# Linear attention and two feed-forward layers on one core: fixed instruction order from block 1 on, and work in smaller pieces

## The chip, the core and the metric

The kernel runs on one core of one Trainium2 chip. The metric is the device time of one execution in microseconds (us). A core has five engines that run side by side, each with an instruction stream of its own: TensorE (PE in the profile; its weight loads are PEld), VectorE (DVE), ScalarE (ACT), GpSimd (POOL) and SyncE (SP), which here issues transfers only. Engines wait for each other by semaphores.

## What is computed

```python
def _attn_ref(q, k, v):                      # 8 batches, 8 heads, 576 positions, 64 wide
    q_s = np.exp(q - np.max(q, axis=-1, keepdims=True))
    q_s = q_s / (np.sum(q_s, axis=-1, keepdims=True) + 1e-09)
    k_s = np.exp(k - np.max(k, axis=2, keepdims=True))
    k_s = k_s / (np.sum(k_s, axis=2, keepdims=True) + 1e-09)
    kv = np.einsum('bhsd,bhse->bhde', k_s, v)
    return np.einsum('bhsd,bhde->bhse', q_s, kv)
...
x = attention, transposed to (4608 tokens, 512)
x = maximum(x @ w_in1, 0) ** 2 @ w_out1      # w_in 512 x 2048, w_out 2048 x 512
h = x @ w_in2
x = (h / (1 + exp(-h))) @ w_out2
```

All of it is float32.

## The kernel before

**Numbers in two halves.** TensorE multiplies a rounded float32 type. To keep float32's precision every operand is split into a high part (ScalarE casts it to the rounded type) and a low part (VectorE subtracts the high part from the value), and each product is three matmuls: high x high, high x low, low x high. Splitting is the main work of ScalarE and VectorE. Weights are rounded beforehand (L170 on ScalarE; L171, L174 and L177 on VectorE, for each of two halves of a weight row block).

**Blocks.** Tokens go in nine blocks of 512 (4608 / 512). Block i runs the first matrix product, `layer_in`, in 16 slots (`for n in range(NF)`): a slot makes 128 of the 2048 hidden values with 12 matmuls into one of four PSUM banks named h. `hidden` then does relu (L580, tile g) and square (L581, tile st) on ScalarE, every fourth slot four sums of 512 columns (L567 to L570; on VectorE, in blocks 7 and 8 on GpSimd with 256 columns), and stores to DRAM (g1d). During block i the attention of block i + 1 is made, for four pairs of heads: loads, maximum over k (`kv_max`, with a reduction over partitions on GpSimd), exp of q and k, k times v on TensorE (`kv_mm`), its normalisation (`kv_norm`), q's normalisation (`q_norm`), a transposition of q through DRAM (`q_tr`: VectorE, one store to qd, four loads to qw), q's split into qh (L505, ScalarE) and ql (L506, VectorE), the product `x_mm` (tile xps, L529 to L531) and its split into xh and xl (`x_keep`). A table of slots, `side`, says in which slot each step is written.

**Phases 1 to 3.** The other three products (w_out1, w_in2, w_out2) use a scheme with seven products of half-size blocks in place of eight (PRODUCTS, with weights B11, T3, T2, T1, B21, N4, B22). A weight set (`seven`) is made for each of 8 row blocks: loads, four subtractions (L240 to L243) and seven splits (L249 on ScalarE, L250 on VectorE). Phase 1's sets are made during the blocks, those of phases 2 and 3 during the last unit of the phase ahead; phases 2 and 3 read weights that `round_to_dram` has rounded and stored meanwhile. A phase has five units, four of two blocks (512 columns) and one of one block (256), in the order 0, 1, 2, 4, 3 in phases 1 and 2. A unit is 56 steps (7 products x 8 row blocks) of six matmuls (`step`, `mm3`). Inputs are loaded 14 steps ahead and split six steps ahead (`stream`: `a_load`, `a_split`, tiles al and ah). In phase 2 each group of seven steps ends in PSUM banks a, b, c and d, read out by `after`: L748 (u + b) and L749 (c + u) after the third product, L752 after the fourth, and so on, then silu, sums and stores. The matmul of product N4, the sixth, adds to bank c again and so has to wait for L749.

**What sets the order.** The kernel is written as a Python program whose statements give the source order. A scheduler then places each engine's instructions; it starts from the source order and lets an instruction pass another where it expects the other to wait. SBUF is handed out as 89 rooms of 128 x 512 (`room`, `back`), and a room that is given back goes to the end of a queue.

## Time and profile before

| | |
|---|---|
| median of 3 runs | 1740.39 us (1737.68 to 1742.43) |
| the profiled execution | 1736.66 us |
| its span, first to last instruction | 1734.9 us |
| TensorE / VectorE / ScalarE / GpSimd busy | 91% / 71% / 50% / 21% of the span |
| mean granted TensorE clock | 0.960 of full speed |

The profile is one execution. Its clock column tells what share of full speed TensorE was granted; the records show two levels, 1.00 (2.4 GHz) and 0.5 (1.2 GHz). Block 0 ends 105 us after the start, block 8 at 584, phase 1 at 965, phase 2 at 1382, phase 3 at 1728.

### The profile page before, as it was taken

What the parts mean: (1) busy time and instruction counts of PE and PEld (TensorE: products, weight loads), DVE (VectorE), ACT (ScalarE), POOL (GpSimd) and SP (SyncE); (2) the same over time, 40 slices, a digit from 0 to 9 for tenths busy, and PEclk for the clock granted to TensorE, in tenths of its full rate; (3) what the DMA queues carried; (4) which work ended last, traced back from release to release, by engine and by line L of the source; (5) the groups of instructions that cost most, each with busy time, mean ns of one, the idle gap of its engine ahead of it and who ended that gap; (6) DMA issues with size and microseconds to landing.
All of it is one profiled execution on the core that took longest, in us unless ns stands there. A gap on an engine that the chain in (4) does not pass through costs nothing. (4 is left out here: it accounts for less than half of the span.)

```text
span 1734.9 us, 25646 instructions
## 1 busy us (share of the span) xinstructions
PE 1587.0 (91%) x7624; PEld 1286.3 (74%) x7624; DVE 1227.1 (71%) x2490; ACT 876.0 (50%) x1981; POOL 369.9 (21%) x628
## 2 busy tenths in 40 slices
PE   6899988989989999999989698989999899999998
PEld 3678766767767788878867477767887688888888
DVE  8876765766677766567677778787778875656565
ACT  7866555555456644444455435343344554444433
POOL 2000000000047600000031343444566600000000
PEclk9999988989989999999899899999999999999999
DMA  8757666666577778796887468677676977776846
GB/s 232 232 191 236 204 193 212 190 217 216 173 255 243 254 255 305 239 322 199 285 271 252 160 236 289 231 272 260 227 241 221 304 233 195 241 239 196 245 130 168
DMA packets 291915, 401.77 MB, mean 232 GB/s; under 512 B 67072, under 2 KB 215296, under 8 KB 290752
## 3 DMA queue, kind: packets, MB, share of 16 engines
q1 hardware_dynamic: 264592, 293.95, 54.8%
q0 software_dynamic: 25824, 105.66, 16.2%
q8 instruction: 61, 1.00, 0.2%
q10 hardware_dynamic: 1360, 0.52, 0.1%
q14 instruction: 78, 0.64, 0.1%
HBM read 226.23 MB, written 173.80 MB: 231 GB/s over the span
## 5 line engine op out<-in xcount | busy, mean ns | idle before, releaser
L671 DVE TENSOR_TENSOR al<-al,ah 128x512 fp32r<-128x512 f32 (+1 forms) x630 | 385.0, 646 | 215.8 <-ACT ah L670 201.8
L670 ACT CAST ah<-al 128x512 fp32r<-128x512 f32 (+1 forms) x630 | 338.6, 576 | 214.5 <-DVE al L671 74.6
L681 PE MATMUL a<-ah,wB 128*128 128x512 f32 (+1 forms) x960 | 288.2, 370 | 7.8 <-ACT u L746 4.1
L555 PE MATMUL h<-xh,wih 128*128 128x512 f32 x576 | 235.7, 415 | 20.2 <-ACT wih L201 8.5
L557 PE MATMUL h<-xh,wil 128*128 128x512 f32 x576 | 234.6, 409 | 1.2 <-DVE wil L202 1.1
L556 PE MATMUL h<-xl,wih 128*128 128x512 f32 x576 | 234.0, 407 | 0.7 <-DVE xl L546 0.7
L681 PEld LDWEIGHTS a<-ah,wB 128*128 128x128 f32 x960 | 176.3, 190 | 39.7 <-ACT u L746 5.2
L681 PE MATMUL c<-ah,wN 128*128 128x512 f32 (+1 forms) x480 | 152.0, 386 | 46.6 <-DVE st L749 46.4
L681 PE MATMUL a<-al,wB 128*128 128x512 f32 (+1 forms) x480 | 178.1, 371 | 0.7 <-DVE al L671 0.6
L681 PE MATMUL d<-ah,wT 128*128 128x512 f32 (+1 forms) x480 | 149.0, 378 | 3.6 <-ACT ah L670 3.5
L555 PEld LDWEIGHTS h<-xh,wih 128*128 128x128 f32 x576 | 113.1, 198 | 51.2 <-ACT xh L545 13.6
L681 PE MATMUL b<-ah,wT 128*128 128x512 f32 (+1 forms) x480 | 146.1, 373 | 3.6 <-ACT ah L670 3.6
L681 PE MATMUL d<-ah,wB 128*128 128x512 f32 (+1 forms) x480 | 147.6, 377 | 0.0
L681 PE MATMUL c<-ah,wT 128*128 128x512 f32 (+1 forms) x480 | 144.7, 369 | 1.5 <-ACT ah L670 1.4
L681 PEld LDWEIGHTS c<-ah,wN 128*128 128x128 f32 x480 | 89.9, 193 | 74.1 <-DVE st L749 56.5
L170 ACT ACTIVATE wraw<-wraw 128x256 int32<-128x256 uint32 x128 | 53.8, 433 | 165.6 <-DMA wraw<-in_moe_w_in_dram 96.2
L580 ACT ACTIVATE g<-h 128x512 f32<-128x512 f32 x144 | 84.6, 594 | 99.1 <-PE h L557 89.8
L557 PEld LDWEIGHTS h<-xh,wil 128*128 128x128 f32 x576 | 113.1, 196 | 27.0 <-DVE wil L202 2.8
L556 PEld LDWEIGHTS h<-xl,wih 128*128 128x128 f32 x576 | 113.6, 197 | 24.8 <-DVE xl L546 1.0
L681 PEld LDWEIGHTS d<-ah,wT 128*128 128x128 f32 x480 | 91.2, 196 | 20.0 <-ACT ah L670 4.9
L739 ACT ACTIVATE st<-st 128x512 f32<-128x512 f32 (+1 forms) x120 | 70.4, 586 | 70.3 <-DVE st L752 28.6
L681 PEld LDWEIGHTS a<-al,wB 128*128 128x128 f32 x480 | 91.0, 190 | 18.0 <-DVE al L671 3.0
(143 smaller groups left out, 2856.3 us busy)
## 6 DMA issues: line engine op xcount, KB each, us to landing
al<-g1d SPq DMA_DIRECT2D x224, 256.0 KB, 5.2
al<-g2d SPq DMA_DIRECT2D x224, 256.0 KB, 3.4
g1d<-st SPq DMA_DIRECT2D x56, 896.0 KB, 4.3
g2d<-st POOLq DMA_DIRECT2D x64, 512.0 KB, 3.4
g2d<-st POOLq DMA_DIRECT2D x112, 256.0 KB, 3.7
wraw<-in_moe_w_in_dram SPq DMA_DIRECT2D x64, 256.0 KB, 4.8
wraw<-in_moe_w_out_dram SPq DMA_DIRECT2D x64, 256.0 KB, 4.3
g1d<-st POOLq DMA_DIRECT2D x16, 896.0 KB, 5.0
```

The costliest lines, as they stand in the source:

```text
L170: nc.scalar.activation(lw, lw.bitcast(U32), AF.Copy, scale=2.0 ** -29)
L555: nc.tensor.matmul(h, wih[f][:, o], xh[i, c], start=(c == 0), stop=False)
L556: nc.tensor.matmul(h, wih[f][:, o], xl[i, c], start=False, stop=False)
L557: nc.tensor.matmul(h, wil[f][:, o], xh[i, c], start=False, stop=(c == KC - 1))
L580: nc.scalar.activation(g, h, AF.Relu)
L670: nc.scalar.copy(hi[:, o], f32(lo)[:, o])
L671: nc.vector.tensor_tensor(lo[:, o], f32(lo)[:, o], f32(hi)[:, o], op=ALU.subtract)
L681: nc.tensor.matmul(p, a, b, start=first and m == 0, stop=last and m == 2, skip_group_check=cont)
L739: nc.scalar.activation(at_(s), at_(s), AF.Silu)
```

## The change

Three things are changed. A wrapper around each engine marks every instruction that is written from block 1 on so that it keeps the source's order on its engine (block 0 and what is ahead of it are left to the scheduler). Attention's steps are cut at the change of engine (`kv_sub` from `kv_exp`, `kv_low` from `kv_norm`, `q_max` from `q_exp`, `q_back` from `q_tr`, `q_low` from `q_split`, `x_low` from `x_keep`) and a table gives each piece its slot; side steps are written ahead of `hidden` of their slot. Weight sets and the roundings to DRAM are generators that give up control after every half rounded, every two subtractions and every split, so that their pieces come one to a slot or step; when they begin is set anew (`WHEN`, and limits on free rooms less those owed). Each engine has the same number of instructions of each kind as before.

```diff
+    class InOrder:
...
+            def call(*a, **kw):
+                got = fn(*a, **kw)
+                if pinned[0] and got is not None:
+                    tc.keep_in_program_order(got)
+                return got
...
-    def rounded(ph, raw, add=None):
+    def rounding(ph, raw, to):
         u = room(F32, "wu")
         for h, t in enumerate(raw):
...
-        back(*raw)
+            back(t)
+            yield
...
-    def round_to_dram(ph, f, raw):
-        u = rounded(ph, raw)
-        nc.gpsimd.dma_start(out=wd[ph, f], in_=u)
-        back(u)
+    def round_to_dram(ph, f):
+        raw = raw_load(ph, f)
+        owed[0] += 1
+        for _ in range(8 if ph == 2 else 4):
+            yield
+        to = []
+        owed[0] -= 1
+        yield from rounding(ph, raw, to)
+        yield
+        gp.dma_start(out=wd[ph, f], in_=to[0])
+        back(to[0])
...
     def seven(ph, x, engine):
...
         engine.tensor_tensor(t1, b12, b11, op=ALU.subtract)
         engine.tensor_tensor(t3, b22, b12, op=ALU.subtract)
+        yield
         engine.tensor_tensor(t2, b22, t1, op=ALU.subtract)
         engine.tensor_tensor(n4, b21, t2, op=ALU.subtract)
-        yield
+        for _ in range(1 if ph == 1 else 4):
+            yield
...
             W[ph, x, n] = w[name]
-            if n == 3:
-                yield
+            yield
...
+    ORDER = (
...
+        (q_tr, 4, 3), (q_back, 4, 4), (kv_norm, 4, 5), (kv_low, 4, 6), (q_split, 5, 7),
+        (q_low, 5, 8), (x_mm, 6, 9), (x_keep, 6, 10), (x_low, 6, 11),
+    )
...
-        for pr, s in enumerate((0, 3, 6, 9) if i == 0 else (-6, -2, 2, 6)):
+        for pr, s in enumerate((0, 3, 6, 9) if i == 0 else (-8, -4, 0, 4)):
...
-    WHEN = [(2, 4), (4, 4), (6, 4), (7, 4), (7, 10), (8, 0), (8, 5), (8, 10)]
+    WHEN = [(1, 8), (3, 8), (5, 8), (7, 0), (7, 0), (7, 8), (8, 0), (8, 4)]
...
+            pinned[0] = i > 0
             h = layer_in(i, fs[n])
...
+            if i > 0:
+                for fn, a in side.get((i, n), ()):
+                    fn(*a)
             hidden(i, n, h)
...
-            if making is not None and (i >= B - 1 or n % 2 == 0):
-                making = None if next(making, 0) == 0 else making
+            if late or n % 2 == 0:
+                making[:] = [x for x in making if next(x, 0) != 0]
...
-    while n1 < NG or making is not None:
-        if making is None:
-            making = seven(1, n1, nc.gpsimd)
+    while n1 < NG or making:
+        if n1 < NG and len(making) < 2 and len(rooms) >= 13 + 11 * len(making):
+            making.append(seven(1, n1, gp))
             n1 += 1
-        making = None if next(making, 0) == 0 else making
+        making[:] = [x for x in making if next(x, 0) != 0]
...
-            a, b = ((n % 14 == 3, n % 14 == 10) if ph == 1 else (
-                (j < NG - 2 and x == 2), (0 < j < NG - 1 and x == 1)
-            ))
...
+        if ph < 3 and not done and nw[ph + 1] < NF and len(rooms) - owed[0] >= 3 and (
+            n % 13 == 3 if ph == 1 else ((u != LAST_LONG[0] or j > 2) and j < NG - 2 and x == 0)
+        ):
+            doing.append(round_to_dram(ph + 1, nw[ph + 1]))
```

What it does to the order is shown at three places. In these rows the changed kernel's line is always L73, the wrapper's; the instruction is known by its tiles. wraw, wu and wt are tiles of the weight rounding and of a set's subtractions; wB, wT and wN are parts of a weight set.

The first is ScalarE in the blocks. Before, in the stretch that ran from 337.67 us, around the end of block 4:

```order
L170 ACTIVATE wraw<-wraw 128x256 x3
L249 CAST wB_3829<-wu 128x256
L170 ACTIVATE wraw<-wraw 128x256
L580 ACTIVATE g<-h 128x512
L581 ACTIVATE st<-g 128x512
L249 CAST wB_3950<-wu 128x256
L249 CAST wB_3944<-wu 128x256
L249 CAST wT_3838<-wt 128x256
L249 CAST wT_3832<-wt 128x256
L249 CAST wT_3835<-wt 128x256
L372 ACTIVATE kvs<-kvps,rc 64x64
L505 CAST qh<-qw 128x512
```

The changed kernel at the end of block 4, where the same weight set gets its first split:

```order
L73 CAST qh<-qw 128x512
L73 ACTIVATE g<-h 128x512
L73 ACTIVATE st<-g 128x512
L73 ACTIVATE g<-h 128x512
L73 ACTIVATE st<-g 128x512
L73 CAST wB_3961<-wu 128x256
L73 ACTIVATE kvs<-kvps,rc 64x64 x2
L73 ACTIVATE q<-q 128x512
L73 ACTIVATE g<-h 128x512
L73 ACTIVATE st<-g 128x512
L73 CAST xh<-xps 128x256
```

Before, q's cast (qh) stands behind a whole weight set and a kvs copy; now it is the first ScalarE instruction of its slot, and the slots after it hold one split each second slot.

The second is VectorE at the start of phase 2, first group of seven steps. Before:

```order
L748 TENSOR_TENSOR u_10006<-b,u_10006 128x512
L250 TENSOR_TENSOR wB_9994<-wB_9994 128x256
L250 TENSOR_TENSOR wN_10060<-wt,wN_10060 128x256
L250 TENSOR_TENSOR wB_9996<-wB_9996 128x256
L171 TENSOR_SCALAR wu<-wraw 128x256 x2
L174 SCALAR_TENSOR_TENSOR wu<-wraw,wu 128x256 x2
L177 ISA wu<-wraw,wu 128x512 x2
L749 TENSOR_TENSOR st<-c,u_10006 128x512
L752 TENSOR_TENSOR st<-d,st 128x512
L758 TENSOR_TENSOR st<-c,u_10006 128x512
```

Now:

```order
L73 TENSOR_TENSOR u_9975<-b,u_9975 128x512
L73 TENSOR_TENSOR st<-c,u_9975 128x512
L73 TENSOR_TENSOR st<-d,st 128x512
L73 TENSOR_TENSOR wB_9906<-wB_9906 128x256
L73 TENSOR_TENSOR wT_10016<-wt,wT_10016 128x256
L73 TENSOR_TENSOR st<-c,u_9975 128x512
L73 TENSOR_TENSOR wT_10027<-wt,wT_10027 128x256
L73 TENSOR_TENSOR st<-d,u_9975 128x512
L73 TENSOR_TENSOR st<-st 128x512 x3
```

The addition that reads bank b and the one that reads bank c now follow each other; the splits stand behind the third addition, and the rounding is gone from here.

The third is ScalarE where the blocks end and phase 1 begins. Before, from shortly ahead of the last relu but one's square (al and ah are phase 1's inputs):

```order
L249 CAST wB_6272<-wu 128x256
L249 CAST wB_6290<-wu 128x256
L670 CAST ah<-al 128x512
L580 ACTIVATE g<-h 128x512
L670 CAST ah<-al 128x512
L581 ACTIVATE st<-g 128x512
L249 CAST wT_6275<-wt 128x256
L249 CAST wT_6278<-wt 128x256
L249 CAST wN_6287<-wt 128x256
L670 CAST ah<-al 128x512 x5
L170 ACTIVATE wraw<-wraw 128x256 x2
L670 CAST ah<-al 128x512 x4
```

Now, from behind the last relu and square and eleven more splits; the casts of ah are those of step 6 and on:

```order
L73 CAST wB_6231<-wu 128x256
L73 CAST wN_6234<-wt 128x256
L73 CAST wB_6237<-wu 128x256
L73 ACTIVATE wraw<-wraw 128x256 x4
L73 CAST wB_6272<-wu 128x256
L73 CAST wT_6275<-wt 128x256
L73 CAST wT_6278<-wt 128x256
L73 CAST wT_6281<-wt 128x256
L73 CAST wB_6284<-wu 128x256
L73 CAST wN_6287<-wt 128x256
L73 CAST wB_6290<-wu 128x256
L73 CAST ah<-al 128x512 x8
```

Before, three splits of the last weight set stand between the last square and the casts of ah; now 14 splits of two sets (the last three are shown) and the four roundings and seven splits of the eighth set stand there. VectorE has the other half of each in the same order.

## Rows read from the trace of the kernel before

**Rows 1.** The page: busy us, share of the span and instructions, by engine.

```profile
PE 1587.0 (91%) x7624; PEld 1286.3 (74%) x7624; DVE 1227.1 (71%) x2490; ACT 876.0 (50%) x1981; POOL 369.9 (21%) x628
```

**Rows 2.** Stage by stage: window and length; busy us (instructions) PE, PEld, DVE, ACT, POOL; clock; DMA share, GB/s.

```profile
0.00:104.90 104.90, 76.33 (x413) 54.44 (x413) 89.66 (x276) 80.06 (x270) 14.89 (x60) 0.95 0.75 220
104.90:207.50 102.60, 102.60 (x582) 82.01 (x580) 70.64 (x176) 60.41 (x140) 9.92 (x46) 1.00 0.70 225
207.50:536.50 329.00, 288.02 (x1400) 222.59 (x1399) 215.34 (x535) 177.31 (x443) 48.42 (x115) 0.91 0.63 206
536.50:584.40 47.90, 45.98 (x195) 37.31 (x195) 38.46 (x62) 29.00 (x65) 37.23 (x48) 0.96 0.75 251
584.40:667.00 82.60, 78.43 (x338) 64.09 (x337) 57.70 (x104) 41.51 (x85) 13.31 (x18) 0.98 0.80 260
667.00:871.50 204.50, 199.38 (x1010) 170.04 (x1009) 137.65 (x286) 89.91 (x200) 9.72 (x18) 0.97 0.81 271
871.50:965.00 93.50, 84.50 (x339) 65.27 (x338) 73.87 (x131) 55.51 (x120) 29.03 (x30) 0.95 0.77 248
965.00:1070.70 105.70, 82.47 (x338) 64.90 (x337) 76.89 (x135) 39.09 (x76) 38.08 (x56) 0.92 0.64 231
1070.70:1241.30 170.60, 158.07 (x674) 126.25 (x673) 131.36 (x218) 72.36 (x139) 75.22 (x107) 0.99 0.70 252
1241.30:1287.40 46.10, 42.82 (x338) 41.18 (x337) 34.97 (x74) 20.06 (x51) 31.28 (x47) 1.00 0.68 231
1287.40:1381.60 94.20, 82.45 (x337) 65.61 (x337) 78.70 (x125) 48.86 (x109) 58.47 (x80) 0.93 0.74 258
1381.60:1686.50 304.90, 304.90 (x1346) 252.22 (x1345) 196.87 (x315) 144.35 (x242) 4.34 (x6) 1.00 0.73 215
```

**Rows 3.** TensorE's waits in blocks 3 to 7: total us, times, longest.

```profile
PE xps L529 <- ACT qh L505: 22.8, 9, 4.8
PE xps L530 <- DVE ql L506: 6.9, 9, 2.5
```

**Rows 4.** TensorE's waits in phase 2, the same columns.

```profile
PE c L681 <- DVE st L749: 46.4, 25, 12.8
```

**Rows 5.** Timeline of ScalarE around the start of block 5: start, us, what, idle before.

```profile
337.67 1.10 ACT L170 ACTIVATE wraw<-wraw 128x256 int32<-128x256 uint32 x3
...
340.14 0.58 ACT L580 ACTIVATE g<-h 128x512 f32<-128x512 f32 x1
340.75 0.63 ACT L581 ACTIVATE st<-g 128x512 f32<-128x512 f32 x1
...
342.29 1.08 ACT L249 CAST wT<-wt 128x256 fp32r<-128x256 f32 x3 [0.29 <-DVE wt L240]
345.97 0.31 ACT L372 ACTIVATE kvs<-kvps,rc 64x64 fp32r<-64x64 f32 x1 [2.60 <-DVE rc L365]
346.18 0.61 ACT L505 CAST qh<-qw 128x512 fp32r<-128x512 f32 x1
```

**Rows 6.** Timeline of VectorE in the first group of phase 2.

```profile
978.32 1.08 DVE L250 TENSOR_TENSOR wT<-wt,wT 128x256 fp32r<-128x256 f32 x3
979.32 0.68 DVE L748 TENSOR_TENSOR u<-b,u 128x512 f32<-128x512 f32 x1
...
987.63 0.29 DVE L171 TENSOR_SCALAR wu<-wraw 128x256 int32<-128x256 int32 x1 [6.63 <-DMA wraw<-in_moe_w_out_dram]
...
990.39 0.68 DVE L749 TENSOR_TENSOR st<-c,u 128x512 f32<-128x512 f32 x1
```

**Rows 7.** GpSimd, 470 to 600 us, by shape: count, busy us, mean ns, idle before.

```profile
L567 POOL TENSOR_TENSOR st<-st 128x256 f32<-128x256 f32 x16 | 13.8, 863 | 50.2 <-DMA g1d<-st 34.8 <-ACT st L581 15.4
...
L240 POOL TENSOR_TENSOR wt<-wu 128x256 f32<-128x256 f32 x5 | 4.3, 861 | 1.7 <-DVE wu L177 1.7
```

**Rows 8.** VectorE, 965 to 1160.4 us, by shape, the same columns: two operations of a rounding.

```profile
L174 DVE SCALAR_TENSOR_TENSOR wu<-wraw,wu 128x256 int32<-128x256 int32 x24 | 9.8, 415 | 0.1
...
L171 DVE TENSOR_SCALAR wu<-wraw 128x256 int32<-128x256 int32 x24 | 6.3, 289 | 22.7 <-DMA wd<-wp 13.1 <-DMA wraw<-in_moe_w_out_dram 7.6 <-ACT wraw L170 2.0
```

More of the change, by code (lines that the diff above doesn't have):

```diff
@@ L60, with __init__, __getattr__ @@
     nc = tc.nc
+    pinned = [False]
+    class InOrder:
+        def __init__(self, engine):
+            self.engine = engine
+        def __getattr__(self, name):
+            fn = getattr(self.engine, name)
+            def call(*a, **kw):
[3 more added lines that the diff above has]
+                return got
+            return call
+    ve, ac, gp, sp, pe = (
+        InOrder(e) for e in (nc.vector, nc.scalar, nc.gpsimd, nc.sync, nc.tensor)
+    )
     P = 128
@@ L186, in rounded @@
             back(u)
-            return to
-        return u
+            u = v
+        to.append(u)
+    def rounded(ph, raw):
+        to = []
+        for _ in rounding(ph, raw, to):
+            pass
+        return to[0]
     wih, wil, raw1 = {}, {}, {}
@@ L218, in seven @@
             raw = [raw_load(ph, f) for f in (x, NG + x)]
-            yield
-            u = [rounded(ph, r) for r in raw]
+            for _ in range(3):
+                yield
+            u = []
+            for r in raw:
+                yield from rounding(ph, r, u)
             b11, b12, b21, b22 = u[0][:, lo_], u[0][:, hi_], u[1][:, lo_], u[1][:, hi_]
-            yield
             t = [room(F32, "wt") for _ in range(2)]
@@ L520, in x_mm @@
                 for o, x in zip(parts(ps, p0, p1), parts(w, p0, p1)):
-                    nc.tensor.matmul(o, kvf[pr], x, start=True, stop=True)
+                    pe.matmul(o, kvf[pr], x, start=True, stop=True)
             else:
@@ L589, in hidden @@
             if half:
-                sums(lambda s: t[:, s], nc.gpsimd)
+                sums(lambda s: t[:, s], gp)
         elif n % 4 == 3:
-            sums(lambda s: sets[0][:, :, s], nc.vector)
+            sums(lambda s: sets[0][:, :, s], ve)
         if half:
@@ L662, in a_load @@
             src = (x2d if ph == 2 else g2d)[u][c]
-            nc.sync.dma_start(out=f32(lo)[:, 0:w], in_=src[:, slot])
+            sp.dma_start(out=f32(lo)[:, 0:w], in_=src[:, slot])
         xs[ph, u, n, c] = [None, lo]
@@ L817, in run @@
         name, j = what[:-1], int(what[-1])
[L818 to L821 removed]
+        fns = code[name]
+        for fn in fns if isinstance(fns, tuple) else (fns,):
+            fn(*((fs[j],) if name in ("w", "round", "split") else (0, j)))
     warm = [spool.tile([P, 1], F32, tag="rc", name="warm", bufs=3) for _ in range(2)]
[L825 to L829 removed]
+    ve.memset(warm[0], 0.0)
+    gp.partition_all_reduce(warm[1], warm[0], P, bass_isa.ReduceOp.max)
+    kv_load(0, 0, ac)
+    r_load(0, 0, ac)
+    ac.activation(warm[0], warm[0], AF.Exp)
     for what in first_loads:
@@ L918, in catch_up @@
         while not need():
-            if not doing or len(doing) < 2 and todo:
+            if not doing or len(doing) < 3 and todo:
                 begin()
@@ L956 @@
             un = LAST_LONG[LAST_LONG.index(u) + 1]
-            while m_next < 7 and len(rooms) >= 2 + (2 if j == NG - 1 else 0):
+            while m_next < 7 and len(rooms) - owed[0] >= 4 + (j == NG - 1 and x < 6):
                 doing.append(factor(un, m_next))
@@ L960 @@
                 m_next += 1
-        while todo and len(rooms) >= todo[0][0] + (6 if ph == 2 and j > 4 else 4) and len(doing) < 3:
+        while todo and len(rooms) - owed[0] >= todo[0][0] + (4 if ph == 2 and j > 4 else 2):
             begin()
```

346 lines of the change are left out of this document (174 added, 172 removed).

## The prediction

> **What bounds the kernel now.** I read the page first, then the busy time of each engine stage by stage, then TensorE's waits, then the timeline around the longest of them. TensorE is busy for 91% of the span and VectorE for 71% [rows 1], but no single engine is the bound everywhere, and the stages show it. The four 512-wide units of phase 3 are the yardstick: TensorE never pauses, its granted clock is 1.00, and 224 steps take 304.90 us, so a step of six matmuls costs 1.36 us and a unit of 56 steps 76.2 us. Blocks 1 and 2 are the other yardstick: 102.60 us without a pause, 51.3 us a block, VectorE busy for 70.64 of it. Against these two rates the rest is late: blocks 3 to 7 take 329.0 us where five at 51.3 us would take 256.5 (72.5 over), the first unit of phase 1 82.6 (6.4 over), its last unit 93.5 (17.3 over), the units of phase 2 with 512 columns 105.7, 170.6 for two, and 94.2 (29.5, 18.2 and 18.0 over) [rows 2]. That is 162 us of late TensorE, and in all of these stretches the granted clock is below 1.00, so part of it is matmuls at 1.2 GHz after a pause.
>
> What the late stretches wait for is two things. In blocks 3 to 7 the matmuls of x_mm wait for the split of q: 22.8 us for its high part on ScalarE and 6.9 us for its low part on VectorE [rows 3]. In phase 2 it is one instruction: the matmul of product N4 into bank c waits 46.4 us in 25 places for VectorE's L749, which reads that bank out [rows 4]. Neither is late for want of data. At 346.18 us the high part of q is cast; ScalarE had stood at roundings and casts of a weight set, and then at a kvs copy that itself waited 2.60 us [rows 5]. At 990.39 us L749 runs, and L748 before it was done at 980.0; in between stood more weight splits and a rounding whose raw weights landed 6.63 us too late [rows 6]. So these stretches are bound by the order of the queues of ScalarE and VectorE.
>
> **The change, part by part.** Every engine gets the same number of instructions as before, so nothing is removed or added; all terms are waits. The terms start from the profiled execution's 1736.66 us (span 1734.9), 3.7 us under the median of the runs.
>
> *Blocks 1 to 7, 431.6 us.* q's cast now stands first in its slot, three slots after q comes back, and a weight set's pieces stand one to every second slot [the first order excerpt]. So the two waits above lose their cause. What is late next is VectorE: the three sets made during blocks 3 to 7 are spread over blocks 1 to 7, which levels its load at (70.64 + 215.34) / 7 = 40.9 us a block against 51.3 of TensorE, 80%, with a round trip to ScalarE or GpSimd in each slot. Bounds: 51.3 us a block (359) and the 65.8 us that blocks 3 to 7 take now (461). I take 53.5, near the first, because blocks 1 and 2 run at full rate with the same round trips and only 5.6 us a block less of VectorE: 374.5, **-57** (-72 to +29).
>
> *Block 0, 104.9 us:* pieces for block 2 start two slots earlier, in a stretch where VectorE is busy for 89.66 us [rows 2]; **+2** (0 to +4).
>
> *Block 8 and the first unit of phase 1.* This is where the new order looks worse. When the blocks end, 14 splits of two weight sets and the whole of the eighth, its four roundings too, stand on ScalarE and VectorE ahead of the split of step 6's input [the third excerpt]; before it was three splits. From the last h matmul: relu and square 0.58 + 0.63 us [rows 5]; on GpSimd four sums and behind them the seventh set's four subtractions, 8 x 0.86 [rows 7], so 8.1 us; its last two splits at 0.36 [rows 6], 8.8; four roundings of the eighth set on VectorE at 0.29 + 2 x 0.41 = 1.1 us each [rows 8], 13.2; three subtractions, 15.8; two splits and the cast of step 6's input (0.61, as q's), 17.1. TensorE has steps 0 to 5, 8.2 us. So it idles for 8.9 us. The clock's share is taken from the first unit of phase 2, where 23.2 us of pauses go with 6.3 us more of TensorE's busy time than the yardstick: 0.27 us for each us idle, 2.4 here. Unit 1.0 then takes 87.5 us instead of 82.6: **+5** (-6, if the eighth set is made before TensorE gets there, to +12); block 8 **-1**.
>
> *The rest of phase 1 but its last unit:* 204.5 us, 11 over the yardstick; mostly DMA, which keeps its sizes: **-3** (-11 to 0). *Its last unit:* three of eight weight sets move out of it and the others come one split a step; VectorE's 73.87 us fall by some 8; 93.5 to 80.5, **-13** (-17 to -5).
>
> *Phase 2.* In its first unit only the fourth to sixth group still rounds weights, each load four steps ahead of its rounding, and L749 stands right behind L748 [the second excerpt]: the 12.8 us wait goes. The late weight sets stand there with 21 splits of 0.36 us where 9 stood; five roundings of 2.2 us leave. 105.7 to 82, **-24** (-29 to -12). In the next two units roundings move from ahead of L748 and L749 to between the fourth and sixth product, where VectorE has 3.7 us of work in 5.4 us: 170.6 to 160.5, **-10** (-18 to 0). The half-wide unit takes over three roundings, 7 us on a VectorE that is busy for 34.97 of 46.1: **+2** (-5 to +4). The last keeps VectorE at 78.70 us less three sets, above 70 in 76.2: 94.2 to 86, **-8** (-18 to 0).
>
> *Phase 3* starts with two weight sets unfinished that step 7 needs: **+2** (0 to +8). Its further units run at the yardstick and stay.
>
> Sum: -57 + 2 - 1 + 5 - 3 - 13 - 24 - 10 + 2 - 8 + 2 = -105. 1736.7 - 105 = 1631.7, and with the median's 3.7 us 1635 us.
>
> **The rivals.** *VectorE sets the pace.* With 40.9 us of work a block and waits of its own it could take 61 us, not 53.5, and phase 2 keep half of its 42 us: then blocks give 4.6 instead of 57 us, phase 2 21, and the time is 1635 + 52 + 21 = 1708 us. For it: in blocks 3 to 7 VectorE idled (329.0 - 215.34) / 5 = 22.7 us a block. Against: much of that idling was itself behind the late casts [rows 3, 5].
>
> *Slower than before: waits stand in line.* With the order fixed nothing can pass an instruction that waits, on any engine. Relu of a slot stands behind q's exp, that behind VectorE's subtraction, that behind the previous slot's sums, which wait for ScalarE's square. The trace shows the size of such a jam: L749 was ready at 980.0 and stood 10.4 us behind a late load [rows 6]. If each slot of blocks 1 to 7 closes this ring, all else as forecast (-48), the time passes that of before when they cost 48 us more than now, 68.5 us a block, 28 of them VectorE idle. One unhidden pair of a ScalarE and a VectorE operation (0.61 + 0.68 us) in each of 16 slots is 21 us, 72 us a block: 1740 + 72 - 48 = 1764 us. The Trainium skill (PSUM — Partial Sum Buffer, Engine vs sequencer instructions) says that the queues of ScalarE, VectorE and GpSimd are strict first in, first out; the 10.4 us agree, and by it alone this rival would follow from any late operand. Against: four h banks let TensorE run three slots, some 9 us, ahead of relu.
>
> *All of it works:* blocks at 51.3, last units at the yardstick, the start of phase 1 as now: -57 becomes -72, +5 becomes 0, phase 2 gains another 20: 1595 us.
>
> *The change does nothing:* excluded, since the rows on ScalarE and VectorE differ where the waits are.
>
> **How the numbers follow.** The forecast 0.60 (1605 to 1675), VectorE's pace 0.18, all of it 0.10, waits in line 0.10, and 0.02 that losses and gains cancel. The predicted time is 1635 us. From 1585 to 1715 leaves out most of the slower case and a little at the low end. Less than 0.3%, 5 us, can't be told from no change: faster 0.88, same 0.02, slower 0.10.
>
> **What would show it.** Right: in blocks 3 to 7 less than 8 us of waits of xps for qh and ql (29.7 now) and a granted clock above 0.97; in phase 2 waits for the read-out of bank c below 15 us (46.4 now), none over 3; at step 6 of phase 1 one wait of 7 to 12 us for the cast of its input. Wrong: VectorE above 90% busy through the blocks with TensorE waiting for xl or ql (its pace), or ScalarE's relu starting several us after its h in every slot with all engines idle (waits in line). The forecast falls if blocks 1 and 2 become slower than 56 us each.

## The result and the profile after

The changed kernel takes 1711.48 us (median of four runs, 1709.19 to 1714.45) against 1740.10 us for the kernel before on the same chip: a ratio of 0.9837, 95% interval 0.9816 to 0.9857. It is faster by 28.6 us where 105 were forecast; 1711 lies inside the range and 76 us above the predicted time.

The page's line of busy time after the change, which answers to [rows 1]:

```profile
PE 1570.9 (92%) x7624; PEld 1281.2 (75%) x7624; DVE 1234.8 (72%) x2490; ACT 879.1 (51%) x1981; POOL 370.1 (22%) x628
```

The same work is done (the instruction counts are those of before) in 24.5 us less span. Where it was gained and lost is seen stage by stage, as in [rows 2]: block 0, blocks 1 and 2, blocks 3 to 7, block 8, then the units of phase 1 (first, next three, last), phase 2 (first, next two, half-wide, last) and the first of phase 3.

```profile
0.00:115.40 115.40, 82.35 (x432) 58.52 (x433) 94.76 (x292) 83.57 (x277) 14.86 (x55) 0.93 0.72 207
115.40:234.50 119.10, 107.41 (x594) 86.01 (x593) 84.07 (x207) 67.43 (x171) 8.54 (x48) 0.97 0.68 221
234.50:524.00 289.50, 263.59 (x1369) 211.05 (x1368) 202.20 (x475) 164.01 (x396) 40.99 (x114) 0.96 0.66 220
524.00:567.50 43.50, 43.50 (x193) 36.05 (x192) 24.73 (x43) 29.79 (x63) 34.75 (x49) 1.00 0.88 311
567.50:665.60 98.10, 81.79 (x337) 66.04 (x336) 74.09 (x136) 49.91 (x102) 16.40 (x22) 0.90 0.69 220
665.60:867.90 202.30, 196.73 (x1009) 167.80 (x1008) 144.18 (x292) 95.49 (x199) 9.72 (x18) 0.99 0.82 270
867.90:944.10 76.20, 76.20 (x338) 63.13 (x337) 66.98 (x121) 49.37 (x105) 29.61 (x24) 1.00 0.89 288
944.10:1028.30 84.20, 79.04 (x338) 63.99 (x337) 62.86 (x99) 31.88 (x65) 40.11 (x56) 0.98 0.62 232
1028.30:1199.90 171.60, 162.50 (x673) 126.99 (x672) 139.79 (x229) 74.42 (x145) 76.61 (x109) 0.98 0.73 266
1199.90:1252.80 52.90, 45.58 (x337) 43.24 (x335) 39.92 (x93) 21.90 (x62) 33.20 (x50) 0.94 0.70 237
1252.80:1347.10 94.30, 82.81 (x338) 64.24 (x337) 74.71 (x119) 42.85 (x94) 53.87 (x73) 0.96 0.73 262
1347.10:1433.20 86.10, 79.95 (x338) 64.60 (x337) 60.35 (x98) 45.52 (x87) 11.44 (x13) 0.94 0.68 200
```

Blocks 3 to 7 fall from 329.0 to 289.5 us, but blocks 1 and 2, which had run without a pause, rise from 102.6 to 119.1: together 408.6 instead of 431.6, where 374.5 were forecast. The last unit of phase 1 is at the yardstick (76.2) and the first of phase 2 gains 21.5 us. Against that block 0 (+10.5), the first unit of phase 1 (+15.5), the half-wide unit of phase 2 (+6.8) and the first of phase 3 (+9.6) are longer.

TensorE's, ScalarE's and VectorE's waits in blocks 1 to 7 after the change (total us, times, longest):

```profile
PE xps L73 <- DVE ql L73: 36.0, 22, 3.5
...
ACT kvs L73 <- DVE rc L73: 136.0, 23, 8.0
...
DVE xl L73 <- ACT xh L73: 24.6, 10, 3.9
DVE wu L73 <- ACT wraw L73: 24.2, 8, 3.4
DVE wB L73 <- ACT wB L73: 19.1, 5, 6.3
DVE wT L73 <- ACT wT L73: 15.4, 5, 4.2
```

The wait for q's high part [rows 3] is gone, and the one for its low part, 6.9 us in blocks 3 to 7 before, has grown to 36.0. Behind it ScalarE and VectorE wait for each other: ScalarE stands 136.0 us at the kvs copy for VectorE's rc (the sum and reciprocal by which kvs is scaled), VectorE 83 us at xl and at weight pieces for ScalarE's cast.

TensorE's waits in the first unit of phase 1, then in phase 2, then in the first unit of phase 3:

```profile
PE a L73 <- ACT ah L73: 11.7, 1, 11.7
PE a L73 <- DVE al L73: 4.4, 1, 4.4
...
PE c L73 <- DVE st L73: 16.1, 15, 4.1
PE b L73 <- DVE al L73: 6.7, 4, 2.0
PE b L73 <- ACT ah L73: 3.4, 4, 1.0
...
PE a L73 <- DVE wB L73: 6.1, 2, 4.0
```

The wait for the read-out of bank c [rows 4] has fallen from 46.4 to 16.1 us. New are the waits for the inputs' splits at the start of phase 1 (16.1 us) and of phase 2's units (ah and al at bank b), and for wB in phase 3.

### The profile page after: what moved, and what is told of

The parts are those of the page before. It is cut to its first block, busy times and chain, and to the rows that moved or that the text cites. A ratio compares the mean times of both kernels' runs of the same rounds, so it can differ in the third digit from the quotient of the medians.

```text
span 1710.4 us, 25752 instructions
## 1 busy us (share of the span) xinstructions
PE 1570.9 (92%) x7624; PEld 1281.2 (75%) x7624; DVE 1234.8 (72%) x2490; ACT 879.1 (51%) x1981; POOL 370.1 (22%) x628
## 3 DMA queue, kind: packets, MB, share of 16 engines
q0 software_dynamic: 25824, 105.66, 16.1%
## 5 line engine op out<-in xcount | busy, mean ns | idle before, releaser
L73 ACT CAST ah<-al 128x512 fp32r<-128x512 f32 (+1 forms) x630 | 347.6, 578 | 234.2 <-PE d L73 71.1
L73 DVE TENSOR_TENSOR al<-al,ah 128x512 fp32r<-128x512 f32 (+1 forms) x630 | 372.5, 644 | 88.5 <-ACT ah L73 86.5
L73 PE MATMUL a<-ah,wB 128*128 128x512 f32 (+1 forms) x960 | 295.3, 376 | 20.9 <-ACT ah L73 11.7
L73 PE MATMUL h<-xh,wih 128*128 128x512 f32 x576 | 236.4, 411 | 15.5 <-ACT wih L73 14.8
L73 PE MATMUL h<-xl,wih 128*128 128x512 f32 x576 | 233.0, 405 | 1.6 <-DVE xl L73 1.6
L73 PE MATMUL h<-xh,wil 128*128 128x512 f32 x576 | 232.7, 405 | 0.2
L73 DVE TENSOR_TENSOR st<-st 128x512 f32<-128x512 f32 (+1 forms) x272 | 206.7, 771 | 24.9 <-ACT st L73 16.6
L73 PEld LDWEIGHTS a<-ah,wB 128*128 128x128 f32 x960 | 180.3, 194 | 54.8 <-ACT ah L73 12.2
L73 PE MATMUL a<-al,wB 128*128 128x512 f32 (+1 forms) x480 | 181.2, 378 | 7.9 <-DVE al L73 7.7
L73 ACT ACTIVATE st<-st 128x512 f32<-128x512 f32 (+1 forms) x120 | 70.7, 589 | 223.4 <-DVE st L73 120.2
L73 PE MATMUL c<-ah,wN 128*128 128x512 f32 (+1 forms) x480 | 149.3, 380 | 16.2 <-DVE st L73 16.1
L73 POOL TENSOR_TENSOR st<-st 128x256 f32<-128x256 f32 (+1 forms) x104 | 113.6, 1099 | 168.0 <-ACT st L73 153.1
L73 PE MATMUL b<-ah,wT 128*128 128x512 f32 (+1 forms) x480 | 145.0, 370 | 3.4 <-ACT ah L73 3.4
L73 PE MATMUL c<-ah,wT 128*128 128x512 f32 (+1 forms) x480 | 145.6, 370 | 2.4 <-ACT ah L73 2.4
L73 PE MATMUL d<-ah,wB 128*128 128x512 f32 (+1 forms) x480 | 145.5, 372 | 1.8 <-ACT ah L73 1.8
L73 PE MATMUL d<-ah,wT 128*128 128x512 f32 (+1 forms) x480 | 145.8, 372 | 0.0
L73 PEld LDWEIGHTS h<-xh,wih 128*128 128x128 f32 x576 | 113.0, 196 | 43.3 <-ACT wih L73 16.5
L73 PEld LDWEIGHTS h<-xh,wil 128*128 128x128 f32 x576 | 112.6, 196 | 26.7 <-DVE wil L73 1.9
L73 PEld LDWEIGHTS h<-xl,wih 128*128 128x128 f32 x576 | 112.7, 196 | 24.9 <-DVE xl L73 2.5
L73 POOL DMA_DIRECT2D g2d<-st x200 | 111.3, 561 | 87.7 <-ACT st L73 66.8
L73 PEld LDWEIGHTS c<-ah,wN 128*128 128x128 f32 x480 | 89.2, 192 | 41.2 <-DVE st L73 25.7
L73 PEld LDWEIGHTS a<-al,wB 128*128 128x128 f32 x480 | 93.1, 194 | 25.8 <-DVE al L73 10.1
```

The costliest lines, as they stand in the source:

```text
L73: got = fn(*a, **kw)
```

## The experiments

Lengths of the stages, in us, in the profiled execution of each run, from the start of the stage's first matmul to that of the next stage's. b0 is block 0, 1.3 is unit 3 of phase 1, and so on; the columns are in order of time. The last column is the ratio of times to the kernel before with its 95% interval. Phase 3's other four units take 276.8 to 277.5 us in every run.

| run | b0 | b1 to b7 | b8 | 1.0 | 1.1, 1.2, 1.4 | 1.3 | 2.0 | 2.1, 2.2 | 2.4 | 2.3 | 3.0 | ratio |
|---|---|---|---|---|---|---|---|---|---|---|---|---|
| before | 104.9 | 431.9 | 47.6 | 82.6 | 204.5 | 93.4 | 105.8 | 170.5 | 46.1 | 94.3 | 76.4 | 1 |
| after | 115.4 | 408.6 | 43.5 | 98.1 | 202.3 | 76.2 | 84.1 | 171.7 | 52.9 | 94.3 | 86.0 | 0.984 (0.982 to 0.986) |
| beforepin | 108.7 | 470.9 | 46.2 | 89.0 | 204.0 | 90.8 | 99.8 | 178.1 | 52.6 | 89.9 | 83.2 | 1.036 (1.033 to 1.039) |
| unpin | 108.8 | 407.8 | 43.5 | 86.8 | 207.4 | 87.7 | 87.4 | 172.8 | 48.4 | 101.3 | 78.1 | 0.988 (0.985 to 0.991) |
| kvs | 116.2 | 398.0 | 43.5 | 98.2 | 200.3 | 76.2 | 84.7 | 171.3 | 53.3 | 93.5 | 87.6 | 0.979 (0.977 to 0.981) |
| deconly | 114.0 | 382.1 | 43.5 | 98.5 | 201.0 | 76.2 | 84.0 | 171.5 | 52.7 | 93.5 | 86.1 | 0.970 (0.968 to 0.972) |
| dec | 111.2 | 370.9 | 43.5 | 99.0 | 202.5 | 76.2 | 84.1 | 171.3 | 53.8 | 94.3 | 86.0 | 0.963 (0.961 to 0.965) |
| decfree | 107.5 | 406.4 | 43.6 | 84.1 | 212.3 | 86.1 | 87.7 | 172.3 | 47.3 | 100.8 | 78.6 | 0.985 (0.982 to 0.988) |
| sums | 111.0 | 413.4 | 43.5 | 98.0 | 202.3 | 76.2 | 83.8 | 171.3 | 52.8 | 94.3 | 86.4 | 0.987 (0.984 to 0.989) |
| decsums | 114.0 | 384.2 | 43.5 | 99.0 | 204.1 | 76.2 | 84.7 | 171.3 | 53.0 | 93.5 | 86.2 | 0.971 (0.969 to 0.973) |
| b0 | 108.7 | 407.8 | 43.5 | 99.0 | 200.6 | 76.2 | 83.8 | 171.4 | 52.8 | 94.3 | 86.1 | 0.982 (0.979 to 0.984) |
| early | 110.7 | 412.4 | 43.5 | 92.2 | 202.9 | 76.2 | 83.9 | 171.4 | 52.4 | 94.3 | 86.3 | 0.983 (0.980 to 0.985) |
| ve | 111.9 | 379.2 | 43.5 | 89.4 | 200.4 | 76.2 | 84.5 | 171.3 | 53.7 | 93.4 | 87.7 | 0.964 (0.962 to 0.967) |
| yields2 | 113.1 | 409.1 | 43.5 | 98.5 | 201.0 | 76.2 | 85.5 | 172.3 | 49.4 | 94.0 | 84.6 | 0.982 (0.980 to 0.984) |
| limits | 110.6 | 408.2 | 43.5 | 98.8 | 204.7 | 76.7 | 84.9 | 170.5 | 51.1 | 94.5 | 77.6 | 0.982 (0.980 to 0.984) |
| lift | 111.8 | 372.2 | 52.5 | 84.4 | 201.6 | 78.7 | 86.5 | 168.5 | 46.8 | 89.9 | 76.5 | 0.949 (0.947 to 0.951) |

The runs that keep the changed kernel's block 0 spread from 110.6 to 116.2 us there, so of after's +10.5 some 5 can be scatter.

### The two parts of the change

*beforepin*: the kernel before with the wrapper alone. *unpin*: the changed kernel with its steps, pieces and slots, but without the fixed order:

```diff
-            pinned[0] = i > 0
+            pinned[0] = False
```

> The kernel before with one part of the change alone: every instruction from block 1 on keeps the source's order of the kernel before; no step is cut and no slot moved. If the fixed order gives the gain by itself (the scheduler's choices were what made q's cast and the read-out of bank c late), the time falls to 1690 to 1720 us. If the order is only worth something with the steps cut to it, instructions now wait in line in the old source order, and the time rises above 1740 us; I expect 1760 to 1850 us, with blocks 1 to 7 well above their 431.6 us.

> The changed kernel without its fixed order: steps, pieces and slots as in the change, the scheduler free to move instructions. If waits standing in line are what blocks 1 to 7 lost (theory of the ring), the scheduler takes some of them out, and the blocks fall from 408 us towards 375: 1680 to 1695 us in all. If VectorE's load sets the pace of the blocks, they stay at about 408 and the time at 1705 to 1720. If the fixed order is what made the gain of phase 2, the waits for bank c come back (46 us before) and the time is 1725 to 1745.

The fixed order alone costs 3.6% (1797 us, as expected): blocks 1 to 7 take 470.9 us. The cut steps alone gain about as much as the whole change (0.988 against 0.984; the intervals just overlap), and by other stages: without the fixed order the last unit of phase 1 (87.7) and the last of phase 2 (101.3) lose, with it the starts of phases 1 and 3 (98.1 and 86.0 against 86.8 and 78.1). The blocks are at 408 either way and the time at 1717 us, as the theory of VectorE's pace had it; the runs on weight pieces below decide against it.

### The blocks: pace, order or ring

*kvs*: ScalarE's two copies of kv_norm become a step of their own, a slot after rc; kv_low follows a slot later.

```diff
-        (q_tr, 4, 3), (q_back, 4, 4), (kv_norm, 4, 5), (kv_low, 4, 6),
+        (q_tr, 4, 3), (q_back, 4, 4), (kv_norm, 4, 5), (kv_high, 4, 6), (kv_low, 4, 7),
```

> The changed kernel with one step cut again: ScalarE's two kvs copies come one slot after VectorE's sum and reciprocal rc on which they wait (and kv_low a slot later), so that relu no longer stands behind a copy that waits. After: ScalarE stands 136 us at kvs for rc, in 23 of 28 places, and TensorE waits 36 us for ql. Theory of the ring: blocks 1 to 7 fall by 15 to 40 us, from 408 to 370 to 395, and TensorE's waits for ql below 20 us. Theory of VectorE's order (ql behind the four sums): the wait at kvs goes elsewhere, the blocks lose less than 6 us. Theory of pace: no change, within 5 us.

*sums*: the four sums and their stores are kept for the next slot, behind its side steps.

```diff
...
+            if i > 0:
+                waiting.append(late_sums)
...
+            while waiting:
+                waiting.pop(0)()
             hidden(i, n, h)
...
```

> The changed kernel with the four sums of every fourth slot (2.7 us of VectorE) and their stores written one slot later, behind ql in place of ahead of it. Theory of VectorE's order: each ql comes up to 2.7 us earlier, TensorE's waits for ql (36.0 us, 22 times, at most 3.5) nearly vanish, below 10 us, and blocks 1 to 7 fall by 20 to 35 us. Theory of the ring: ql waits for something else, the waits stay above 20 us, and the gain is below 10 us. Theory of pace: the waits move to xl or h, and the blocks stay within 5 us.

Kvs gives 10.6 us in the blocks, less than the 15 to 40 expected of the ring, and TensorE still waits 29.6 us for ql. Sums brings the waits for ql down to 14.6 us (below 10 was expected), and yet the blocks get no shorter (413.4): the waits moved to xl and to kvps, as the theory of pace had it. But sums changed a second thing. The stores to g1d now come one slot ahead of the loads of k instead of two, and these loads take 6.4 us from issue to landing (median) instead of 3.8; VectorE waits 12.9 us for them, where in after it had no such wait. So sums alone doesn't settle what the place of ql costs. The timeline of kvs in block 4, VectorE, then ScalarE, then TensorE (start, us, what, idle before), shows where VectorE idles:

```profile
297.72 0.69 DVE L73 TENSOR_TENSOR ql<-qw,qh 128x512 fp32r<-128x512 f32 x1
...
306.25 0.42 DVE L73 CUSTOM_DVE_ANT_0 wu<-wraw,wu 128x512 uint16<-128x512 uint16 x1 [2.41 <-ACT wraw L73]
...
310.57 2.71 DVE L73 TENSOR_TENSOR st<-st 128x512 f32<-128x512 f32 x4
313.19 0.69 DVE L73 TENSOR_TENSOR ql<-qw,qh 128x512 fp32r<-128x512 f32 x1
...
300.81 0.63 ACT L73 ACTIVATE q<-q 128x512 f32<-128x512 f32 x1 [4.30 <-DVE q L73]
...
305.81 0.41 ACT L73 ACTIVATE wraw<-wraw 128x256 int32<-128x256 uint32 x1
...
316.28 0.63 ACT L73 ACTIVATE q<-q 128x512 f32<-128x512 f32 x1 [6.92 <-DVE q L73]
...
313.93 0.69 PE L73 MATMUL xps<-ql,kvs 128*128 128x384 f32 x1 [2.42 <-DVE ql L73]
```

From one ql (297.72) to the next (313.19) VectorE needs 15.5 us, and TensorE's four slots 12.8. It is idle in one place only, 2.41 us, for ScalarE's cast of raw weights. That cast (305.81) is late because ScalarE had stood 4.30 us at q's exp for VectorE's subtraction, and afterwards it stands there again for 6.92. This is a ring: a weight piece has both halves in one slot, so VectorE waits for ScalarE, which waits for an earlier instruction of VectorE. Without the 2.41 us VectorE has 13.1 us of work with its gaps for 12.8 of TensorE's: in the slots with weight pieces no wait can be made up.

*dec* (built on kvs) and *deconly* (without it) take the halves apart, with the same instructions: VectorE's half of a weight piece goes out with the next piece, two slots later.

```diff
...
+            def low_part(n=n, name=name):
+                ve.tensor_tensor(
+                    w[name][:, hi_], all_[name], f32(w[name])[:, lo_], op=ALU.subtract
+                )
...
+            if ph == 1:
+                while owing:
+                    owing.pop(0)()
             ac.copy(w[name][:, lo_], all_[name])
...
+            if ph == 1:
+                owing.append(low_part)
...
```

The three VectorE operations of a rounding are put off in the same way. *decfree* is dec without the fixed order; *decsums* is dec with the late sums.

> The kernel of the run before last but one (kvs copies a slot after rc) and, beside that, the two halves of a weight piece taken apart in the blocks: ScalarE's cast of a piece goes out in one piece's slot, VectorE's half of it in the next piece's, two slots later, so that VectorE no longer waits for ScalarE at wu, wB, wT and wN (67 us in all there). VectorE's work stays the same: 12.4 us in four slots that take TensorE 12.8 us. Theory of the ring: VectorE now runs through, blocks 1 to 7 fall from 398 us to 365 to 380, the whole to 1665 to 1683 us (before 1735). Theory of pace (12.4 us of work in 12.8 leaves no room for anything): blocks stay at 390 to 400, the whole at 1690 to 1700.

> The changed kernel with the halves of the weight pieces taken apart alone, kvs copies where the change put them. Two links of the ring are then still closed: ScalarE's copy behind rc in the slot. If the ring needs only one link opened, the blocks are as in the run with both (371 us, 1672 to 1676 in all). If the two add up, they are at 380 to 392 us and the time at 1682 to 1694: the copies alone gave 10.6 us of 408.6, both 37.7.

> The run with the pieces taken apart with no fixed order at all, the scheduler free. If what the blocks need is only the cut of the steps, it is as fast there, 365 to 375 us, and better at the seams (first groups, starts of phases 1 and 3): 1640 to 1660. If the fixed order is what holds the pieces in their slots, the blocks are back at 390 to 410 us, as without it before (408), and the time at 1690 to 1712.

> The run with the pieces taken apart, and the four sums one slot later, behind ql, as in the run of the late sums. There VectorE still waits 32.4 us for ScalarE's square at the sums and TensorE 12.1 us for ql, blocks 1 to 7 take 370.9 us (359 without a pause). Ring and order together: what is left is these waits, and blocks 1 to 7 fall to 361 to 367, the whole from 1672 to 1662 to 1668. Rival: the late sums push xl and the next slots back as they did alone (no gain, other waits for 36 us less of ql): the blocks stay at 369 to 375 and the whole at 1670 to 1676.

Blocks 1 to 7 (windows: start to end, length, then busy us and count of PE, PEld, DVE, ACT, POOL, clock, DMA share, GB/s) in kvs, in dec, and in decfree:

```profile
116.20:514.20 398.00, 368.05 (x1961) 294.68 (x1961) 286.91 (x682) 232.16 (x566) 49.78 (x162) 0.97 0.69 226
```

```profile
111.20:482.10 370.90, 358.64 (x1962) 289.28 (x1962) 288.32 (x682) 231.33 (x566) 49.44 (x163) 1.00 0.74 244
```

```profile
107.50:513.90 406.40, 382.97 (x1941) 296.87 (x1940) 280.10 (x695) 233.79 (x579) 56.82 (x161) 0.96 0.67 224
```

VectorE's busy time is the same in kvs and dec (286.91 and 288.32 us), and the blocks are 27 us shorter, 18 of them less idle time of TensorE and 9 less busy time, at a clock of 1.00 instead of 0.97: not pace, but the ring. The two links add up (10.6 and 26.5 alone, 37.7 together), so there is no single one; both runs came out as that theory had it (1672 and 1683 us). The waits of dec in the blocks:

```profile
PE xps L73 <- DVE ql L73: 12.1, 13, 2.4
...
ACT q L73 <- DVE q L73: 78.7, 19, 5.0
...
DVE wu L73 <- ACT wraw L73: 1.8, 2, 1.1
...
DVE wT L73 <- ACT wT L73: 1.5, 1, 1.5
DVE wB L73 <- ACT wB L73: 1.3, 1, 1.3
```

VectorE's waits for weight casts (wu, wT, wB) are down from 59 us in after and 54 in kvs to 5; that ScalarE still waits 78.7 us for VectorE costs little now: TensorE idles 12.3 us in all there.

Decfree is the other half of the finding: without the fixed order the same pieces take 406.4 us. The scheduler bunches them again: in blocks 1 to 6, 10 of the 28 gaps between the starts of ScalarE's weight pieces are under 1.5 us, in dec none. The fixed order is worth 35 us here, once the order that it fixes has these two links open; 11 of them are TensorE's pauses and 24 its busy time, at 0.96 of full clock. Which of the moved instructions cost it was not tested.

Decsums takes 384.2 us in the blocks, 13 more than dec, where both theories had 375 or less. The late stores again stand closer to the loads. VectorE's first wait in the blocks of decsums, then the loads of k (count, size, median us from issue to landing), first in dec, then in decsums:

```profile
DVE m L73 <- DMA k<-in_k_dram: 41.1, 17, 7.0
```

```profile
k<-in_k_dram SPq DMA_DIRECT2D x21, 256.0 KB, 3.3
```

```profile
k<-in_k_dram SPq DMA_DIRECT2D x21, 256.0 KB, 6.4
```

Dec has no wait of VectorE for k. A step put off makes room on one queue and can crowd another, here that of the transfers; that this is the whole of the 13 us was not tested.

### The starts of phases and units

*b0* starts block 2's attention later (`(-5, -2, 1, 4) if i == 1`). *early* begins the last weight sets of phase 1 earlier. *ve* is dec and early, and moves the sums of blocks 7 and 8 and these sets' subtractions from GpSimd to VectorE.

```diff
-            if n1 < NG and (i, n) >= WHEN[n1] and len(making) < (3 if late else 1):
-                if len(rooms) >= 15 + 7 * len(making):
+            if n1 < NG and (i, n) >= WHEN[n1] and len(making) < (4 if late else 1):
+                if len(rooms) >= (15 + 3 * len(making) if late else 15):
```

> The changed kernel with block 2's attention moved back by three slots for the first pair, two for the second and one for the third, so that fewer of its pieces fall into block 0. If these pieces are what lengthened block 0 (104.9 to 115.4 us), it falls to 105 to 109 us and the whole by 6 to 10 us, unless block 1, where the pieces now stand closer, loses it again. If block 0 is longer because its own steps are cut in another way for the scheduler, it stays at 112 us or more.

> The changed kernel with the last weight sets of phase 1 begun earlier: up to four at a time in block 8, and a limit on free rooms of 15 + 3 a set instead of 15 + 7, so that the eighth set begins in slot 6 of block 8 and only some 12 splits are left when the blocks end. Theory: the wait at step 6 (11.7 us for ah, 4.4 for al) stands behind the making of the eighth set; the first unit of phase 1 then falls from 98.1 to 82 to 87 us and block 8 gains at most 1.5 us: 1692 to 1698 in all. Rival: the wait is for the transfers of the inputs, and stays: 1704 to 1710. In the third case block 8 pays for it: VectorE has 24 us of work there in 43.5, so I expect no more than 3 us.

> Kvs copies a slot after rc, weight pieces taken apart, early weight sets in block 8, and new: the sums of blocks 7 and 8 and the subtractions of phase 1's last weight sets go to VectorE in place of GpSimd. While GpSimd works there, VectorE's operations of 128x256 take 0.83 to 0.96 us in place of 0.28 to 0.43. Theory of contention: GpSimd's 64 sums and 20 subtractions cost VectorE as much as they save it; VectorE takes 84 x 0.36 = 30 us more work over blocks 7 and 8 and phase 1's start, loses the stretching, and the first unit of phase 1 falls from 92 to 99 us to 80 to 88; the whole to 1652 to 1663. Rival: the stretching is chance, VectorE becomes the bound of blocks 7 and 8, which rise above 50 us each, and the whole is 1666 to 1680 (1672 for the run with the pieces apart).

In b0 block 0 takes 108.7 us, 2 to 8 less than in the runs that keep it, and block 1 56.7 instead of 55.0; the ratio can't be told from after's. Early gives 5.9 us of the first unit's 15.5, not the 11 to 16 expected: the inputs' splits now stand behind the same weights at step 0 (one wait of 10.2 us for al) instead of step 6, and blocks 1 to 7 pay some 4 us. Ve is about one reason why the weights take so long there. Two of VectorE's forms (count, busy us, mean ns) in after at the end of block 8 and the start of phase 1, where GpSimd works, then GpSimd's sums there, then the same forms in ve, where GpSimd does none of this:

```profile
L73 DVE SCALAR_TENSOR_TENSOR wu<-wraw,wu 128x256 int32<-128x256 int32 x12 | 7.2, 604 | 0.4
...
L73 DVE TENSOR_SCALAR wu<-wraw 128x256 int32<-128x256 int32 x12 | 5.5, 462 | 0.0
...
L73 POOL TENSOR_TENSOR st<-st 128x256 f32<-128x256 f32 x17 | 13.7, 813 | 3.1 <-ACT st L73 2.4
```

```profile
L73 DVE SCALAR_TENSOR_TENSOR wu<-wraw,wu 128x256 int32<-128x256 int32 x13 | 5.5, 425 | 0.5
...
L73 DVE TENSOR_SCALAR wu<-wraw 128x256 int32<-128x256 int32 x12 | 3.4, 286 | 0.0
```

The means, 604 and 462 ns instead of 425 and 286, mix two kinds. In after's trace, six of the twelve operations of the first form run while GpSimd runs one of its additions or subtractions, and take 782 ns; the other six take 425. Of the second form five take 715 ns beside GpSimd and seven 282 without it. The Trainium skill (SBUF — State Buffer, Who interferes with whom) says that a VectorE instruction with two SBUF inputs contends with a GpSimd instruction that reads SBUF. The first form has two such inputs and agrees; the second has one, which this sentence does not cover.

Yet moving the work gains nothing: the first unit of phase 1 is 9.6 us shorter than in dec, more than half of which early gave by itself, blocks 1 to 7 are 8.3 us longer (block 7 takes 57.0 us instead of 48.0), and ve's ratio is dec's. The theory of contention holds for the durations and fails for the time; 1673 us is what the rival had.

*yields2* shortens the distance of load and split in phases 2 and 3 to two steps; *limits* also lets factors and sets begin with fewer free rooms, and has one step instead of two ahead of a set's splits. *lift* is dec, limits' weight sets with their old factors, and no fixed order at the seams:

```diff
+        pinned[0] = n >= 16 and (ph != 2 or 0 < j < NG - 1)
```

and from slot 8 of block 8 on.

> The changed kernel with the load and the split of phase 2's factors two steps apart instead of four, and the same for the loads, subtractions and splits of phase 2's and 3's weight sets. If the first groups of phase 2's units (16.5, 16.5, 11.2 and 16.0 us; 10.3, 9.8, 7.7 and 8.9 before) and the start of phase 3 (86.0 us; 76.4 before) are late because each piece now takes more steps from its begin to its end, the four groups fall by 3 to 6 us each and phase 3's first unit by 4 to 9, 16 to 30 us in all: about 1680 to 1695. If they are late because rooms come free too late to begin, nothing changes in them (within 4 us): 1703 to 1710. If a load needs the four steps, new waits for transfers appear at al and wB.

> The changed kernel with its limits on free rooms let down in phase 2 (a factor begins with 2 rooms free that are not owed, in place of 4; a weight set with its 9, in place of 11 or 13) and two steps in place of four between a factor's load and its split (a set: 2 and 1 in place of 4 and 4). By the program, six of a unit's seven factors are then split when the unit begins, as before the change; now it is three, while 12 to 13 rooms are free and 8 of them owed. Theory of the limits: the first groups of units 2.1, 2.2, 2.4 and 2.3 (16.5, 16.5, 11.2, 16.0 us) fall to 9.5 to 11 (the half-wide one to 6 to 8), and the start of phase 3 from 86.0 to 77 to 81: 1680 to 1690 in all (1707 to 1712 without). Rival: the pieces themselves are too slow for VectorE whenever they begin; the groups stay above 14 us and the time above 1700.

> The run with the pieces taken apart (1672 us), with the fixed order lifted at three kinds of places: from the middle of block 8 to step 16 of phase 1, in the last group of each unit of phase 2 and in the first group of the next, and phase 2's and 3's weight sets take two and one steps in place of four and four between load, subtraction and split and begin with 9 rooms. Theory: at these seams the fixed order itself is the loss; the kernel with no fixed order has first groups of 10.7, 11.1, 7.3 and 11.3 us where the changed one has 16.5, 16.5, 11.2 and 16.0, and a first unit of phase 1 of 86.8 us where it has 98.1. Then the four groups lose 16 to 22 us, phase 1's first unit 9 to 13, phase 3's 7 to 9, and the time is 1630 to 1642 us. Rival: the order gets worse inside the units, as it is without any fixed order (interior groups of 13.7 to 16.0 us), and the time is 1655 to 1670.

The first group of seven steps (42 matmuls, from the first to the next group's first) of units 2.1, 2.2, 2.4 and 2.3 takes 10.3, 9.8, 7.7, 8.9 us before; 16.5, 16.5, 11.2, 16.0 after; 15.0, 16.7, 11.7, 12.8 in beforepin; 10.7, 11.1, 7.3, 11.3 in unpin; 18.9, 18.5, 11.8, 16.4 in yields2; 17.0, 16.0, 11.6, 13.8 in limits; 15.8, 11.3, 7.8, 13.0 in lift. With the fixed order it is long in both kernels, without it short in both; earlier splits (limits) don't cure it, and neither run came near the times that their theories gave (1705.7 us in both). The timeline of after at the end of unit 2.0, VectorE, then ScalarE, then TensorE:

```profile
1029.72 1.29 DVE L73 TENSOR_TENSOR al<-al,ah 128x512 fp32r<-128x512 f32 x2 [1.21 <-ACT ah L73]
1030.93 0.68 DVE L73 TENSOR_TENSOR st<-d,u 128x512 f32<-128x512 f32 x1
1031.53 3.09 DVE L73 TENSOR_TENSOR st<-st 128x512 f32<-128x512 f32 x3
1034.54 3.69 DVE L73 TENSOR_TENSOR al<-al,ah 128x512 fp32r<-128x512 f32 x6
...
1031.64 0.63 ACT L73 ACTIVATE st<-st 128x512 f32<-128x512 f32 x1 [1.44 <-DVE st L73]
1032.18 1.12 ACT L73 CAST ah<-al 128x512 fp32r<-128x512 f32 x2
...
1035.27 0.50 PE L73 MATMUL b<-al,wT 128*128 128x512 f32 x1 [1.93 <-DVE al L73]
```

TensorE stood at bank b until 1035.27 for al. Its split is one of the six at 1034.54, behind three sums (3.09 us) of the unit that ends and an addition, and that stood behind splits for which VectorE waited 1.21 us, while ScalarE's casts stand behind a silu that waits for VectorE (1.44 us): again two queues that wait for each other. This is after's wait only. In limits those for al and ah are gone from the four groups, and TensorE waits 0.6 to 3.9 us in each for ScalarE's copy out of bank a, as in beforepin (1.0 to 3.1).

The start of phase 3 is another matter: there limits (77.6) cures what unpin cures (78.1). It was not the steps between a set's pieces alone: yields2, with two steps instead of four, stays at 84.6. What limits has beyond that is the lower limit on free rooms and one step less; the two were not taken apart.

Lift takes 1646.96 us, 5.1% less than before and 3.6% less than the changed kernel by the two ratios (0.9486 / 0.9837); it lies between its theory (to 1642) and the rival (from 1655). Against dec the first unit of phase 1 is 14.6 us shorter, and the four first groups 12.9 in all (60.8 to 47.9), not 16 to 22. The first unit of phase 3 is 9.5 shorter, about what limits' sets gave by themselves. Not all of it came as expected: block 8 takes 52.5 us instead of 43.5 with the order lifted from its middle, and unit 2.1's first group stays at 15.8. Its waits are 2.0 us there and the granted clock is 0.78; why it pauses is open.

## Why the prediction was wrong, and where it was right

**Blocks 1 to 7 (-57 forecast, -23 measured): the step that failed.** "I take 53.5, near the first, because blocks 1 and 2 run at full rate with the same round trips". They did so while the scheduler could let other instructions pass a waiting one: with the old source order fixed (beforepin) block 1 takes 62.4 us, and no weight piece is in it. And they did so with hardly a weight piece. In the kernel before, ScalarE's first cast of raw weights behind block 0 stands at the very end of block 2:

```profile
204.57 0.44 ACT L170 ACTIVATE wraw<-wraw 128x256 int32<-128x256 uint32 x1
```

With the order fixed, each round trip inside a slot is a place where both queues can stand, and blocks 1 and 2 themselves rose to 55.0 and 64.1 us (under 56 each was the condition). The mean of 40.9 us of VectorE a block hid the rest: it was 31.0 to 45.6 us by block, and in kvs 13.1 us for 12.8 in the slots with weight pieces. The mechanism was the slower rival's, waits in line, at 58 us a block instead of its 72; the loop was closed at weight pieces and kvs copies. Q's exp behind VectorE's subtraction was a link of it, as that rival had it (4.30 us in kvs); the sums' wait for the square was small (14.5 us in all in after). Opening two links gives 370.9: the forecast of 374.5 fits an order without them, and the kernel's order had both.

That 1711 us is also near the 1708 of the rival "VectorE sets the pace" is chance: VectorE was busy for 286 of 408.6 us in the blocks, 70%, not above 90, and with the same work they take 370.9.

**Phase 2 after its first unit (-10, +2, -8 forecast; +1, +7, 0 measured).** The gain inside the units is there: bank c's waits are 16.1 us (below 15 forecast), the longest 4.1 (none over 3 forecast). The step left out was the seam: the four first groups cost 23.5 us more than before, and the fixed order is what made them long (beforepin, unpin); new waits there had been priced at nothing.

**First unit of phase 1 (+5 forecast, +15.5 measured).** The wait at step 6 came as forecast in place and kind, 11.7 us for 8.9, but its size by luck, since both terms of the difference were too small. VectorE, GpSimd, then TensorE in after (the last h matmul ends at 567.5):

```profile
572.76 3.98 DVE L73 TENSOR_TENSOR al<-al,ah 128x512 fp32r<-128x512 f32 x3
...
579.46 2.07 POOL L73 TENSOR_TENSOR wt<-wu,wt 128x256 f32<-128x256 f32 x2
...
595.05 0.79 PE L73 MATMUL a<-ah,wB 128*128 128x512 f32 x1 [11.74 <-ACT ah L73]
```

The cast of step 6's input was done 27.5 us after the last h matmul, not 17.1. The seventh set's subtractions on GpSimd ended 14.0 us after it, not 8.1, as VectorE still made that set's roundings, its operations stretched beside GpSimd; then the rest of 14 splits stood there until 18.3, where two had been counted (8.8); the eighth set's four roundings took 5.4 us, not 4.4. TensorE in turn needed 15.8 us for steps 0 to 5, not 8.2: another wait, of 4.4 us for al, stands in step 1, and the clock was low. In all it is busy for 81.8 us where the yardstick is 76.2, 5.6 us for 16.1 us idle, not 2.4.

**First unit of phase 3 (+2 forecast, +9.6 measured):** right in kind, two waits for weight parts (6.1 us), too small; lower limits on rooms, with one step less, cure it (limits), shorter pieces alone don't (yields2). **Block 0** (+2): +6 to +11, for a cause that stays open.

**Right within 5 us:** block 8 (-4), the middle of phase 1 (-2), its last unit (-17, where all of the bound came true) and the first unit of phase 2 (-22). There an instruction was moved out of another's way and no new wait came; the terms that failed had priced new waits at nothing or too low.
